# FFN1 block products, pre-added exp tiles, masks on GpSimd and wide w_in transfers in an attention + ELU-FFN kernel

## The chip, the cores and the metric

The program runs on one core of a Trainium2 chip. The metric is the device time of one execution in microseconds. A "stage" below is the time from the first FFN2 matmul of one token tile to that of the next, read from the trace.

## The reference, cut

```python
# q, k, v: 8 batches x 8 heads x 576 tokens x 64; 16 beacon keys and values in front
scores = scale * np.matmul(q, k_all.transpose(0, 1, 3, 2))      # 576 x 592
scores = np.where(causal, -1000000000.0, scores)                # beacons always visible
a = np.exp(scores - max);  a /= a.sum(-1, keepdims=True) + 1e-09
x = np.matmul(a, v_all)                                         # -> 4608 tokens x 512
h = x @ w_in                                                    # 512 x 2048    (FFN1)
g = np.where(h > 0.0, h, np.exp(np.minimum(h, 0.0)) - 1.0)      # ELU
return (g @ w_out).astype(np.float32)                           # 2048 x 512    (FFN2)
```

## The kernel before

The 4608 tokens form ten tiles: two of 256 tokens (0 and 1), then eight of 512 (2 to 9). The kernel runs every engine in a fixed order, written as a list of words. `F.b.0` means "step F on tile b, unit 0", and `z`, `b`, `c`, `d` stand for tile or batch number b-1, b, b+1, b+2. One pass through the list is a stage: FFN1 of tile b, FFN2 of tile b-1 and attention of the next batch, woven together.

FFN1 has 16 units per tile. A unit is four matmuls of 512 columns into one of two PSUM banks (tag `hps`), then exp and relu on ScalarE and one combine on VectorE, min(exp(h)-1, relu(h)), which is ELU:

```python
    def F(t, i):                                  # 16 units per 512-token tile
        h = hp[t, i] = bank("hps", name="hps") ...
        for n_ in range(512 // w):
            for cc in range(NCC):                 # 4 chunks of 128 of d_model
                nc.tensor.matmul(out=h[:, n_, :], lhsT=w_in16[:, cc, P * fc:P * (fc + 1)],
                                 rhs=xt[k][:, cc, ...], start=(cc == 0), stop=(cc == NCC - 1))
    def e(t, i):  # ScalarE:  eb = exp(h)
    def u(t, i):  # ScalarE:  rb = relu(h)
    def kk(t, i): # VectorE:  half(t, i) = min(eb - 1, rb)
```

FFN2 (step Q) already uses seven block products in place of eight (112 matmuls of 256 columns); its operand sums (Z) are on VectorE, its partial sums are copied out by step J. Softmax row sums (step L) are matmuls of the exp tiles with ones, four heads side by side, each summed over five key chunks in PSUM:

```python
    def quad(b, g, qa, qe, t, half, first):       # half is None: row sums, else value products
        for n, (j, a, e, c) in enumerate(pcs):    # key chunks
            for i in range(4):                    # four heads, 32 columns of the array each
                nc.tensor.matmul(out=t[32 * i:32 * (i + 1), ...],
                    lhsT=ones[0:kc[j], :] if half is None else v16[...],
                    rhs=ets[b, p][0:kc[j], i % 2, c:c + e - a], ...)
```

The causal masks (m) are multiplications by a triangle on VectorE. Every tile and row sum above runs in the order of the word list, one list per engine.

The softmax here doesn't subtract the row's maximum and nothing guards it: scores larger than these inputs give would overflow.

## Time and profile before

| | before |
|---|---|
| time, median (three runs; range) | 351.61 us (351.27 to 355.36) |
| first FFN2 block product (end of the start) | 105.73 us |
| stages of tiles 3, 4, 5, 6 | 35.57, 35.55, 35.55, 35.55 us |
| stages of tiles 7, 8, 9 (attention runs out) | 34.41, 26.04, 25.18 us |
| last FFN2 | 16.2 us |

The first row is the metric; the other rows are from the one profiled execution, whose span is 349.78 us, and add up to it. The prediction below shows the page lines.

### The profile page before, as it was taken

The numbers are of one execution on the slowest core, as the hardware profiler recorded it, in microseconds if no ns is written. First come the engines' busy times: TensorE is split into PE (matmuls) and PEld (weight loads), VectorE is DVE, ScalarE is ACT, GpSimd is POOL, SyncE is SP. The second block draws the span as 40 slices with busy tenths as digits, with TensorE's granted clock in tenths as the row PEclk, the third lists the DMA queues.
The fourth block names the chain that finished last, engine by engine and source line by source line (L and its number), as shares of the span: only waits on it lengthen the run. The fifth ranks groups of instructions, "written<-read, shape, count | busy, mean of one in ns | idle before, by whom it ended". The sixth has DMA issues, their size and how long they took to land.

```text
span 349.8 us, 8839 instructions
## 1 busy us (share of the span) xinstructions
PE 335.8 (96%) x3651; PEld 204.6 (59%) x3651; DVE 242.3 (69%) x514; ACT 281.2 (80%) x473; POOL 91.7 (26%) x120
## 2 busy tenths in 40 slices
PE   8887998989999999999999999999999999999995
PEld 3454655444455656656665666565665666666684
DVE  2672689689798758675867676767776767667661
ACT  1893998679868997999799979997999676777731
POOL 8877446493009107300640050000000000000000
PEclk9998999999999999999999999999999999999999
DMA  9999999999709998993799359300100010010022
GB/s 117 147 150 141 185 182 174 155 140 154 136 33 152 138 114 79 175 137 73 74 172 154 66 63 182 84 2 32 62 32 2 32 60 32 30 63 30 32 90 91
DMA packets 136232, 34.67 MB, mean 99 GB/s; under 512 B 119040, under 2 KB 135680, under 8 KB 136192
## 3 DMA queue, kind: packets, MB, share of 16 engines
q0 software_dynamic: 102080, 18.51, 67.7%
q1 hardware_dynamic: 33536, 15.47, 20.1%
q8 instruction: 28, 0.46, 0.5%
q10 hardware_dynamic: 576, 0.13, 0.2%
q14 instruction: 12, 0.10, 0.1%
HBM read 37.22 MB, written 15.34 MB: 150 GB/s over the span
## 4 chain that ended last, share of the span: by engine, by line
PE 81%; ACT 5%; DMA 4%; DVE 4%; POOL 3%; issue 1%; DVEq 0%; ACTq 0%; POOLq 0%
PE hps L432 34%; PE ops L542 28%; PE ut L322 6%; PE sc L285 6%; DMA w_in<-in_moe_w_in_dram 4%; PE lt L322 3%; PE ops L478 3%; ACT et L295 2%; ACT e L442 1%; DVE qk L259 1%; POOL kst L134 1%; POOL qst L134 1%; DVE r L464 1%; ACT r L447 1%; POOL v L147 1%
## 5 line engine op out<-in xcount | busy, mean ns | idle before, releaser
L432 PE MATMUL hps<-xT,w_in 128*128 128x512 f16 (+1 forms) x640 | 148.9, 359 | 3.9 <-DMA w_in<-in_moe_w_in_dram 2.5
L457 DVE SCALAR_TENSOR_TENSOR gt<-e,r 128x512 f16<-128x512 f32 x133 | 92.0, 692 | 59.2 <-ACT r L447 54.3
L442 ACT ACTIVATE e<-hps 128x512 f32<-128x512 f32 x144 | 89.3, 621 | 33.7 <-PE hps L432 32.6
L295 ACT ACTIVATE et<-sc 128x832 f16<-128x832 f32 x128 | 106.0, 897 | 2.7 <-PE sc L285 2.6
L542 PEld LDWEIGHTS <-gt 128*128 128x128 f16 x768 | 75.1, 98 | 29.0 <-issue 0.3
L447 ACT ACTIVATE r<-hps 128x512 f16<-128x512 f32 x133 | 82.8, 624 | 5.0 <-PE hps L432 2.5
L432 PEld LDWEIGHTS <-w_in 128*128 128x128 f16 x640 | 56.5, 98 | 50.0 <-issue 7.4
L542 PE MATMUL ops<-wt,gt 128*128 128x256 f16 x384 | 52.5, 273 | 0.0
L542 PE MATMUL ops<-w_out,gt 128*128 128x256 f16 x384 | 51.4, 273 | 0.0
L311 DVE TENSOR_TENSOR et<-et,triu 128x256 f16<-128x256 f16 (+2 forms) x164 | 41.8, 357 | 13.2 <-ACT et L295 11.0
L147 POOL DMA_DIRECT2D v<-in_v_dram x40 | 35.5, 977 | 5.7 <-DMA w_out<-in_moe_w_out_dram 1.7
L499 DVE TENSOR_TENSOR gt<-gt 128x1024 f16<-128x1024 f16 x48 | 32.5, 683 | 0.0
L322 PE MATMUL ut<-et,v 128*32 128x464 f16 (+4 forms) x672 | 23.6, 283 | 1.0 <-DVE qk L263 1.0
L396 DVE TENSOR_TENSOR xT<-ut,rl 128x448 f16<-128x448 f32 (+7 forms) x56 | 22.3, 452 | 2.8 <-ACT rl L364 2.3
L322 PEld LDWEIGHTS <-v 128*32 128x32 f16 (+1 forms) x800 | 17.4, 98 | 11.5 <-issue 4.8
L285 PE MATMUL sc<-qkd 64*128 64x208 bf16 (+5 forms) x320 | 21.5, 252 | 0.0
L142 POOL DMA_DIRECT2D v<-in_beacon_v_dram x8 | 4.3, 536 | 60.1 <-PE ut L322 57.2
L551 ACT COPY sm<-ops 128x512 f32<-128x512 f32 x24 | 16.0, 667 | 5.0 <-PE ops L542 5.0
L558 DVE TENSOR_TENSOR osb<-ops,sm 128x512 f32<-128x512 f32 x24 | 16.4, 683 | 4.3 <-issue 3.7
L285 PE MATMUL sc<-qk 64*128 64x208 bf16 (+10 forms) x208 | 15.4, 246 | 2.8 <-ACT et L295 2.5
L542 PE MATMUL ops<-w_out,s 128*128 128x256 f16 x128 | 17.6, 273 | 0.0
L285 PEld LDWEIGHTS <-qkd 64*128 64x128 bf16 x320 | 11.3, 94 | 10.4 <-issue 8.2
(59 smaller groups left out, 257.3 us busy)
## 6 DMA issues: line engine op xcount, KB each, us to landing
out_dram<-osb SPq DMA_DIRECT2D x36, 256.0 KB, 2.3
v<-in_v_dram POOLq DMA_DIRECT2D x24, 128.0 KB, 6.9
scr<-in_k_dram POOLq DMA_DIRECT2D x5, 576.0 KB, 17.1
scr<-in_q_dram POOLq DMA_DIRECT2D x5, 576.0 KB, 10.3
w_in<-in_moe_w_in_dram POOLq DMA_DIRECT2D x16, 128.0 KB, 6.8
w_out<-in_moe_w_out_dram POOLq DMA_DIRECT2D x4, 512.0 KB, 9.9
v<-in_v_dram POOLq DMA_DIRECT2D x8, 112.0 KB, 5.7
v<-in_v_dram POOLq DMA_DIRECT2D x8, 80.0 KB, 7.0
```

Of the source, the lines that this page charges most:

```text
L147: nc.gpsimd.dma_start(out=vt[b][r0:r0 + n, j, :, :], in_=v[b, :, ilo[j]:ilo[j] + n, :].rearrange("h s d -> s h d"),)
L285: nc.tensor.matmul(out=s[:, h, a - c0:e - c0], lhsT=t[D * h:D * (h + 1), 1, P * j:P * (j + 1)], rhs=t[D * h:D * (h + 1), 0, NB + qa + a - ...
L295: nc.scalar.activation(out=ets[b, p][:, :, GW * g:GW * (g + 1)], in_=sc[b, p, g][:, :, 0:GW], func=AFT.Exp, bias=0.0, scale=SCALE)
L311: nc.vector.tensor_tensor(out=o, in0=o, in1=triu[0:kc[j], :, t0:t0 + e - a], op=ALU.mult)
L322: nc.tensor.matmul(out=t[32 * i:32 * (i + 1), a - qa:e - qa], lhsT=ones[0:kc[j], :] if half is None else v16[0:kc[j], j, h, 32 * half:32 * ...
L396: nc.vector.tensor_tensor(out=x_tile(k)[:, cc, tok - TT * k:to - TT * k], in0=u[:, o:o + to - tok], in1=r[:, o:o + to - tok], op=ALU.mult)
L432: nc.tensor.matmul(out=h[:, n_, :], lhsT=w_in16[:, cc, P * fc:P * (fc + 1)], rhs=xt[k][:, cc, a - TT * k:e - TT * k], start=(cc == 0), sto ...
L442: nc.scalar.activation(out=eb[t, i], in_=flat(hp[t, i]), func=AFT.Exp, bias=0.0, scale=1.0)
L447: nc.scalar.activation(out=rb[t, i], in_=flat(hp[t, i]), func=AFT.Relu, bias=0.0, scale=1.0)
L457: nc.vector.scalar_tensor_tensor(out=half(t, i), in0=eb[t, i], scalar=1.0, in1=rb[t, i], op0=ALU.subtract, op1=ALU.min)
L499: nc.vector.tensor_tensor(out=o_, in0=a_, in1=b_, op=op_)
L542: nc.tensor.matmul(out=xy[t, n_][:, qd, :], lhsT=lw[:, P * qd:P * (qd + 1)], rhs=wt_[:, c, :], start=(first and qd == 0 and c == 0), stop= ...
```

## The change

Intent: take work off TensorE, which sets the end, and put it on engines with room.

- In tiles 4 to 9, three groups of four of the 16 FFN1 units become seven block products each: 28 matmuls of 256 columns in place of 16 of 512. The products accumulate in two PSUM banks; partial sums are copied out and added (K), so h appears in SBUF or in PSUM, and ELU is formed as max(h, min(exp(h), 1) - 1), with the clamp on GpSimd (U).
- Exp tiles are added over key chunks 1 to 4 (D) so that a row-sum group needs 8 matmuls, not 24.
- Some masks (m with `.p`), operand sums and chunk adds go to GpSimd.
- w_in arrives in 16 transfers, each 1024 columns wide (before, 512); the start is reordered, and q and k are staged in fixed buffers.

```diff
-        f_ = slice(512 * c, 512 * (c + 1))
+        f_ = slice(DF // 2 * c, DF // 2 * (c + 1))
         for g in range(2):
-            for t in range(2):
-                nc.gpsimd.dma_start(out=w_in16[:, 2 * g + t, f_], in_=wi_v[:, :, g, t, f_])
+            for i in range(4):
+                nc.gpsimd.dma_start(
+                    out=w_in16[32 * i:32 * (i + 1), 2 * g:2 * g + 2, f_], in_=wi_v[i, :, g, :, f_])
 ... [masks]
+                nc.gpsimd.affine_select(
+                    out=o, in_=o, compare_op=ALU.is_ge, fill=0.0, base=t0,
+                    pattern=[[0, 2], [1, e - a]], channel_multiplier=-1)
 ... [D_: chunk adds]
+        (nc.vector if eng == "v" else nc.gpsimd).tensor_tensor(
+            out=o, in0=t[0:rows, :, a:e] if n == 0 else o, in1=t[0:rows, :, col:col + e - a], op=ALU.add)
 ... [row sums of batches from BD on]
+                    nc.tensor.matmul(
+                        out=t[32 * i:32 * (i + 1), a:e], lhsT=ones,
+                        rhs=(presum if a else ets)[k][:, i % 2, a:e],
+                        start=True, stop=True, skip_group_check=True)
 ... [seven products, partial sums, exp, clamp, maximum]
+    ring = {"hs": [0, fr[0:2]], "sm": [0, fr[2:4]]}
+    def P_(t, g, ph):           # 4 matmuls of 256 columns
+    def K_(t, g, ph, eng="s"):
+        if ph in (0, 2, 3):
+            (nc.scalar.copy if eng == "s" else nc.vector.tensor_copy)(out=fm[t, g, ph], in_=src)
+        else:
+            nc.vector.tensor_tensor(out=hb[t, g, ph], in0=src, in1=fm[...], op=ALU.add)
+    def E_(t, g, ph):           # ScalarE exp of hb (ph 6: of PSUM)
+    def U_(t, g, ph):
+        if ph == 6:
+            nc.scalar.activation(out=r_, in_=hsrc(t, g, ph), func=AFT.Relu, bias=0.0, scale=1.0)
+        else:
+            nc.gpsimd.tensor_scalar(
+                out=r_, in0=eb[t, g, ph], scalar1=1.0, scalar2=1.0, op0=ALU.min, op1=ALU.subtract)
+    def V_(t, g, ph):           # VectorE: max(hb, clamp); ph 6: the old combine
 ... [new word lists: the start; BODY3 (tile 3, makes the weight sums H); BODY (4 to 7); TAIL (8, 9)]
```

## The prediction

> **What bounds the kernel now.** I read the page's busy shares and slices first, then the chain of waits that ended last, then the stages by window, then the timeline of one stage, then GpSimd's and VectorE's timelines side by side.
>
> ```profile
> PE 335.8 (96%) x3651; PEld 204.6 (59%) x3651; DVE 242.3 (69%) x514; ACT 281.2 (80%) x473; POOL 91.7 (26%) x120
> PE   8887998989999999999999999999999999999995
> PE 81%; ACT 5%; DMA 4%; DVE 4%; POOL 3%; issue 1%; DVEq 0%; ACTq 0%; POOLq 0%
> L432 PE MATMUL hps<-xT,w_in 128*128 128x512 f16 (+1 forms) x640 | 148.9, 359 | 3.9 <-DMA w_in<-in_moe_w_in_dram 2.5
> ```
>
> TensorE is busy for 96%, carries 81% of the chain, and what idle it has lies in the first third. So two regions have to be treated apart: a start with holes and a steady part without. The windows (columns: window; length, PE, weight loads, DVE, ACT, POOL busy; clock; DMA share; GB/s) say the same:
>
> ```profile
> 20.00:30.00 10.00, 6.47 (x139) 4.12 (x139) 6.21 (x14) 6.75 (x12) 7.01 (x11) 0.99 1.35 142
> 178.00:213.00 35.00, 35.00 (x383) 21.38 (x378) 24.82 (x55) 32.36 (x56) 5.88 (x11) 1.00 1.14 115
> 284.50:317.00 32.50, 32.50 (x222) 21.47 (x221) 22.10 (x35) 24.05 (x46) 0.00 (x0) 1.00 0.10 34
> ```
>
> From about 106 us on, the program repeats one stage per 512-token tile: FFN1 of tile b, FFN2 of tile b-1 and attention of the next batch; the last two FFN1 tiles have no attention. The chain gives the period and the cost of each piece (start, length):
>
> ```profile
> 182.17 0.82 PE lt L322 x24
> ...
> 204.51 0.97 PE hps L432 x4
> 206.25 0.86 PE hps L432 x4
> ...
> 217.72 0.82 PE lt L322 x24
> ...
> 332.99 13.01 PE ops L542 x119
> ```
>
> The row sums of the same group come 217.72 - 182.17 = 35.55 us apart, all of it TensorE work. A 512-column matmul costs 0.86/4 = 0.216 us, a 256-column one 13.01/119 = 0.109 us, and one group's row sums (24 matmuls, four column groups side by side, 1664 columns) 0.82 us.
>
> ScalarE and VectorE are pipelined, so their cost is the distance of starts, not the length shown:
>
> ```profile
> 249.27 0.69 DVE L457 SCALAR_TENSOR_TENSOR gt<-e,r 128x512 f16<-128x512 f32 x1 [0.34 <-ACT r L447]
> 249.88 0.69 DVE L499 TENSOR_TENSOR gt<-gt 128x1024 f16<-128x1024 f16 x1
> 250.49 0.66 DVE L311 TENSOR_TENSOR et<-et,triu 128x224 f16<-128x224 f16 x2
> 251.19 0.62 ACT L447 ACTIVATE r<-hps 128x512 f16<-128x512 f32 x1
> 251.67 1.65 ACT L295 ACTIVATE et<-sc 128x832 f16<-128x832 f32 x2
> 253.16 0.65 ACT L442 ACTIVATE e<-hps 128x512 f32<-128x512 f32 x1
> ```
>
> VectorE: 0.61 us for 512 fp32 elements or for 1024 fp16 ones. ScalarE: 0.48 us for 512 elements, (253.16 - 251.67)/2 = 0.745 us for a softmax exp of 832. Three masks of 256 fp16 elements ran in 0.63 us, some 0.2 us each.
>
> **What the Trainium skill says.** (1) "TensorE: Matmul & The Clock Gate", Back-to-back issue gap: N/2.4 + 2.5 ns; that is 0.216 and 0.109 us, and the trace agrees to the nanosecond. So halving a matmul costs only some 2.5 ns, and fewer streamed columns are time won. (2) "VectorE: DVE Perf Modes", the perf-mode tier table: tensor_tensor runs at two elements per cycle in 16 bits and one in fp32; the 0.61 us for both sizes agree. (3) "SBUF — State Buffer", Who interferes with whom: a VectorE instruction with two SBUF inputs and a GpSimd instruction that reads SBUF exclude each other for the whole instruction. The trace shows it once, plainly:
>
> ```profile
> 77.76 3.66 POOL L585 COPY qkd<-bkT 128x32 bf16<-128x32 bf16 x1
> 79.74 0.68 DVE L499 TENSOR_TENSOR wt<-w_out 128x1024 f16<-128x1024 f16 x1
> 80.34 0.43 DVE L311 TENSOR_TENSOR et<-et,triu 128x256 f16<-128x256 f16 x2
> 80.70 0.68 DVE L499 TENSOR_TENSOR wt<-w_out,wt 128x1024 f16<-128x1024 f16 x1
> 81.30 0.68 DVE L485 COPY osb<-ops 128x512 f32<-128x512 f32 x1
> ```
>
> A 32-element copy that needs 0.21 us elsewhere took 3.66 us, and ended at 81.42, as soon as VectorE went to an instruction that reads PSUM alone. (4) "GPSIMD Engine Reference", Elementwise: 4497 ns for a two-input fp32 add of 2048, so 2.2 ns per element. No two-input operation runs on GpSimd in the kernel before.
>
> **The change, part by part.**
>
> Block products (tiles 4 to 9, three groups of four of the 16 FFN1 units). Each group: 16 matmuls of 512 columns become 28 of 256. Per tile 48 x 0.216 = 10.37 us become 84 x 0.109 = 9.2 us, so 1.2 us less; six tiles 7.0 us. All of it lies on the engine that sets the end. The price is on the others. Per group there were 4 exp, 4 relu (ScalarE) and 4 combines (VectorE). Now there are 3 ScalarE copies of partial sums, 4 exp and 1 relu (again 8 operations); on VectorE 3 adds from PSUM and 4 combines; and 3 clamps on GpSimd.
>
> Row sums. With chunks 1 to 4 added ahead, one group streams 112 + 464 = 576 columns and not 1664: 0.82 x 576/1664 = 0.28 us, so 0.54 us less, twice per batch, for batches 3 to 7: 5.4 us. The adds are 16 fp16 instructions per batch on VectorE or GpSimd.
>
> Sum on TensorE: 7.0 + 5.4 = 12.4 us: 2.25 us in each of the stages of tiles 4 to 7 (35.55 to 33.3), 1.1 in that of tile 3, 1.2 in each of the last two FFN1 tiles.
>
> Do the others keep up with 33.3 us? Counted from the built program's order, per stage of tiles 4 to 7:
> - ScalarE: 12 exp, 3 relu, 8 copies, 8 exp and relu of the plain quarter, 3 output copies = 34 x 0.48 = 16.3; 16 softmax exps x 0.745 = 11.9; 4 normalisers at about 0.55 = 2.2. Sum 30.4 us (before 31.4).
> - VectorE: 37 operations at about 0.6 (16 combines, 10 partial sums, 7 FFN2 operand sums, 4 outputs) = 22.2; 8 masks x 0.2 = 1.6; 9 chunk adds 3.3; 4 x differences 1.3; scaling 2.8. Sum 31.2 us (before about 23).
> - GpSimd, estimates: 9 clamps at about 0.63 (its two select instructions took 0.29 us for 128 and 0.40 us for 256 elements, extrapolated), 12 selects x 0.4 = 4.8, 7 chunk adds 7.5 and one operand sum 2.3 at the skill's 2.2 ns, copies 0.5: about 21 us that read SBUF; with some 8 us of DMA issue about 29 us.
>
> None exceeds 33.3 alone, but all stand at 87 to 94%, in strict order, with only two PSUM banks for a group and a ring of two for the partial sums. Each product must wait until the partial sum two products back has been copied out. I allow 1 us lost per stage of tiles 4 to 7, 4 us in all. In the stage of tile 3 VectorE has 24 weight sums (0.2 each), 16 chunk adds and 20 masks beside its old work: about 35 us, so its 1.1 us is lost too.
>
> The start. TensorE's work there hardly changes. Before, it is held from 27 to 31 us for w_in, which comes in column quarters; now half of all columns come in eight wide transfers, behind more of q and k, and scores of batch 1 lie before the first FFN1. The holes for w_in are about 5 us; I take 3 us as won, plus or minus 4.
>
> Result: 351.6 - 12.4 + 1.1 + 4 - 3 = 341.3; I say 341.
>
> **Rivals.** First, the shared port becomes the bound. Per stage VectorE has about 20 us of two-SBUF-input work (combines, operand sums, masks, chunk adds) and GpSimd about 21 us of reads. If they exclude each other wholly, that is 41 us against 33.3, partly hidden only under VectorE's 11 us from PSUM. Each of four stages would grow by 3 to 5 us over 35.55, and the time would be 355 to 370. For it: the 3.66 us copy. Against: the clamp's and selects' lengths are extrapolated, reads may be over before an instruction ends, the order puts GpSimd's work beside PSUM adds, and VectorE waiting for a clamp leaves the port free. Second, the copy-out of partial sums becomes TensorE's wait: the stages stay near 35.5, and only the start and the last tiles show a gain, 345 to 350. For it: a product of four matmuls takes 0.44 us, its copy about 0.67 us plus queueing. Against: FFN2 products and scores stand between the products. Third, all engines follow, and the start closes its holes: 333 to 337.
>
> **Range and chances.** The main path gives 336 to 345 and is the likeliest; the second rival lies within 2% and the first above it. With 344.6 as the limit for a gain of 2%: faster 0.66, within 2% 0.19, slower 0.15. Range 332 to 357.
>
> **What would show it.** Right: stages of tiles 4 to 7 some 34 us long with TensorE over 95% busy; row-sum groups of about 0.28 us; 84 products per stage at 0.109 us. The first rival: GpSimd's clamps and adds far longer than 0.6 to 2 us, VectorE's combines waiting for a clamp, TensorE idle for VectorE. The second: TensorE idle in front of products, released by ScalarE's or VectorE's copy-out. The start is right if FFN2's first block product comes at about 103 us, not 106, and no matmul waits for w_in. I would be wrong above all if GpSimd's share in a stage nears 100%.

## More of the kernel before

One more row of the windows, the whole stage of tile 5, is the yardstick for everything that follows (columns: window in us; length; busy us and instructions of PE, weight loads, VectorE, ScalarE, GpSimd; granted clock; DMA share; GB/s):

```profile
176.85:212.40 35.55, 35.55 (x385) 21.64 (x384) 25.21 (x56) 32.91 (x57) 7.03 (x11) 1.00 1.14 114
```

TensorE is busy for the whole stage, ScalarE for 93%, VectorE for 71%; GpSimd hardly works.

## The result, and the profile after

| | before | after |
|---|---|---|
| time, median of four runs each on the same chip | 351.44 us (351.2 to 355.36) | 428.36 us (427.39 to 429.62) |
| span of the profiled execution | 349.78 | 427.92 |
| first FFN2 block product | 105.73 | 101.13 |
| stages of tiles 3, 4, 5, 6 | 35.57, 35.55, 35.55, 35.55 | 38.10, 53.10, 53.11, 52.25 |
| stages of tiles 7, 8, 9 | 34.41, 26.04, 25.18 | 45.79, 37.95, 30.34 |

The changed kernel is correct and much slower: ratio 1.217, 95% interval 1.209 to 1.225. A ratio here is the mean time of one kernel's fast runs over that of the other's of the same rounds, so it is not quite the ratio of the medians that are quoted.

The 78.1 us between the two profiled spans divide as: start -4.6, stage of tile 3 +2.5, stages of tiles 4 to 7 +63.2, last two tiles +17.1 (differences of the rows above). So the start did what it should, and each stage with block products lost 5 to 18 us. One wait of the start before, in which matmuls wait for w_in (us in total, times, longest), is gone after:

```profile
PE hps L432 <- DMA w_in<-in_moe_w_in_dram: 2.5, 2, 1.3
```

The page after (busy shares; the chain of waits by engine; the largest GpSimd group, with busy us, mean ns of one and the idle time before it):

```profile
PE 351.5 (82%) x3700; PEld 230.2 (54%) x3700; DVE 351.8 (82%) x630; ACT 278.9 (65%) x455; POOL 275.0 (64%) x258
...
POOL 34%; PE 25%; DVE 19%; ACT 12%; issue 8%; DMA 1%; DVEq 0%; ACTq 0%; POOLq 0%
L681 POOL TENSOR_SCALAR r<-e 128x512 f16<-128x512 f32 x54 | 108.8, 2032 | 68.6 <-ACT e L672 67.1
```

TensorE fell from 96% busy to 82% and from 81% of the chain to 25%; GpSimd, 26% busy before, now leads the chain with 34%. Its clamps alone are 54 instructions of 2.03 us mean; GpSimd spent another 67.1 us waiting for their input. An engine that is waiting and leading the chain at once is part of a loop, not simply overloaded. By stage (tile 3, tile 5, tile 9; same columns as above):

```profile
101.13:139.23 38.10, 34.98 (x354) 21.22 (x352) 34.63 (x88) 33.93 (x57) 19.72 (x18) 1.00 1.02 95
...
192.33:245.44 53.11, 39.89 (x389) 26.52 (x388) 46.27 (x69) 33.62 (x55) 45.35 (x43) 0.89 0.77 79
...
381.43:411.76 30.33, 25.25 (x206) 19.91 (x204) 25.39 (x38) 17.85 (x32) 19.93 (x10) 1.00 0.11 36
```

In the middle row VectorE is busy 46.3 us and GpSimd 45.4, where I had counted 31 and 29. TensorE's 39.9 us are not more work, since it streams fewer columns than in the old stage; the granted clock was 0.89 here, and 1.00 in the stages of tiles 3 and 9. What lowered it, and what share it has in the loss, was not tested. The waits (waited for; us in total, times, longest) name the loop:

```profile
POOL r L681 <- ACT e L672: 67.1, 20, 9.7
...
DVE gt L694 <- POOL r L681: 20.5, 30, 1.8
PE hps L650 <- DVE kst L663: 17.6, 10, 5.3
PE hps L650 <- DVE qst L663: 17.3, 9, 5.3
```

A product (L650) waits up to 5.3 us for VectorE's addition of a partial sum (L663), the exp (L672) waits for that sum, the clamp (L681) for the exp, VectorE's maximum (L694) for the clamp; and VectorE, in strict order, reaches the next partial sum only after that maximum. A piece of the chain of waits in tile 5's stage shows it (start, length, what):

```profile
225.79 0.54 ACT e L672
...
232.14 1.89 POOL r L681
234.03 1.68 POOL et L322 x3
...
235.90 1.94 POOL r L681
...
237.87 1.94 DVE gt L694
```

The last line is a maximum that takes 0.68 us where GpSimd is idle. The timeline beside it shows why (start, length, engine, line, operation):

```profile
220.87 2.63 DVE L351 TENSOR_TENSOR qk<-et 128x928 f16<-128x928 f16 x1 [0.58 <-POOL et L322]
221.07 1.93 POOL L351 TENSOR_TENSOR qk<-et 128x928 f16<-128x928 f16 x1
...
237.80 2.83 POOL L351 TENSOR_TENSOR qk<-qk,et 128x672 f16<-128x672 f16 x2
237.87 1.94 DVE L694 TENSOR_TENSOR gt<-qst,r 128x512 f16<-128x512 f32 x1 [0.25 <-POOL r L681]
```

A chunk add of 0.63 us (the median of this form) became 2.63 us on VectorE beside a GpSimd add: the exclusion on the shared port that the prediction quoted from the Trainium skill, "SBUF — State Buffer", Who interferes with whom. The trace agrees here. (In the lines that the prediction shows, only GpSimd's copy waited; VectorE's instructions kept their lengths.)

So there are three suspects: the clamp's own length, the port, and a dependence loop with engines too full to run ahead. They have to be told apart by experiments.

### The profile page after: what moved, and what is told of

Read it like the earlier page. It is cut to its first block, busy times and chain, and to the rows that moved or that the text cites. A ratio compares the mean times of both kernels' runs of the same rounds, so it can differ in the third digit from the quotient of the medians.

```text
span 427.9 us, 9235 instructions
## 1 busy us (share of the span) xinstructions
PE 351.5 (82%) x3700; PEld 230.2 (54%) x3700; DVE 351.8 (82%) x630; ACT 278.9 (65%) x455; POOL 275.0 (64%) x258
## 4 chain that ended last, share of the span: by engine, by line
POOL 34%; PE 25%; DVE 19%; ACT 12%; issue 8%; DMA 1%; DVEq 0%; ACTq 0%; POOLq 0%
POOL r L681 19%; PE hps L468 7%; ACT et L303 6%; PE ops L578 5%; POOL et L322 5%; DVE gt L493 4%; POOL qk L351 3%; POOL gt L535 3%; PE hps L650 3%; PE ops L514 3%; DVE gt L694 3%; PE sc L293 2%; DVE gt L535 2%; POOL scr L710 2%; ACT e L672 2%
## 5 line engine op out<-in xcount | busy, mean ns | idle before, releaser
L681 POOL TENSOR_SCALAR r<-e 128x512 f16<-128x512 f32 x54 | 108.8, 2032 | 68.6 <-ACT e L672 67.1
L468 PE MATMUL hps<-xT,w_in 128*128 128x512 f16 (+1 forms) x352 | 72.9, 346 | 9.3 <-DVE kst L663 3.5
L660 ACT COPY kst<-hps 128x512 f32<-128x512 f32 x46 | 26.9, 589 | 40.7 <-PE hps L650 40.3
L468 PEld LDWEIGHTS <-w_in 128*128 128x128 f16 x352 | 32.4, 99 | 37.2 <-issue 14.6
L483 ACT ACTIVATE r<-hps 128x512 f16<-128x512 f32 x56 | 33.7, 610 | 27.8 <-PE hps L468 19.9
L478 ACT ACTIVATE e<-hps 128x512 f32<-128x512 f32 x72 | 43.7, 610 | 3.2 <-PE hps L468 1.6
L493 DVE SCALAR_TENSOR_TENSOR gt<-e,r 128x512 f16<-128x512 f32 x56 | 42.6, 779 | 1.8 <-ACT r L483 1.4
L650 PEld LDWEIGHTS <-w_in 128*128 128x128 f16 x288 | 27.9, 105 | 26.2 <-issue 13.4
L320 DVE TENSOR_TENSOR et<-et,triu 128x256 f16<-128x256 f16 (+3 forms) x119 | 34.5, 323 | 5.3 <-ACT et L303 4.1
L694 DVE TENSOR_TENSOR gt<-qst,r 128x512 f16<-128x512 f32 x27 | 28.0, 1036 | 12.2 <-POOL r L681 12.1
L694 DVE TENSOR_TENSOR gt<-kst,r 128x512 f16<-128x512 f32 x27 | 29.8, 1105 | 8.5 <-POOL r L681 8.4
L650 PE MATMUL hps<-xT,w_in 128*128 128x256 f16 x144 | 24.7, 310 | 9.4 <-DVE kst L663 4.7
L650 PE MATMUL hps<-qst,lo 128*128 128x256 f16 x72 | 12.0, 294 | 21.3 <-DVE kst L663 11.1
L672 ACT ACTIVATE e<-kst 128x512 f32<-128x512 f32 x27 | 17.1, 634 | 16.6 <-DVE kst L663 16.5
L322 POOL TENSOR_SCALAR_AFFINE_SELECT et<-et 128x256 f16<-128x256 f16 (+2 forms) x45 | 27.2, 624 | 0.0
L650 PE MATMUL hps<-qst,w_in 128*128 128x256 f16 x144 | 23.7, 291 | 4.2 <-DVE qst L663 2.3
```

Of the source, the lines that this page charges most:

```text
L320: nc.vector.tensor_tensor(out=o, in0=o, in1=triu[0:kc[j], :, t0:t0 + e - a], op=ALU.mult)
L322: nc.gpsimd.affine_select(out=o, in_=o, compare_op=ALU.is_ge, fill=0.0, base=t0, pattern=[[0, 2], [1, e - a]], channel_multiplier=-1)
L478: nc.scalar.activation(out=eb[t, i], in_=flat(hp[t, i]), func=AFT.Exp, bias=0.0, scale=1.0)
L493: nc.vector.scalar_tensor_tensor(out=half(t, i), in0=eb[t, i], scalar=1.0, in1=rb[t, i], op0=ALU.subtract, op1=ALU.min)
L650: nc.tensor.matmul(out=hx[t, g, n_][:, c, :], lhsT=lw, rhs=rh, start=(first and c == 0 and k_ == 0), stop=(k_ == 1), skip_group_check=True)
L681: nc.gpsimd.tensor_scalar(out=r_, in0=eb[t, g, ph], scalar1=1.0, scalar2=1.0, op0=ALU.min, op1=ALU.subtract)
```

## The experiments

Besides the changed kernel seventeen ran. The times of sixteen and of after, medians of two to six fast runs, each beside the kernel before on the same chip:

| kernel | median us | before | ratio (95% interval) | stage of tile 5, us | result |
|---|---|---|---|---|---|
| after | 428.36 | 351.44 | 1.217 (1.209 to 1.225) | 53.11 | correct |
| clamp_one | 411.83 | 352.63 | 1.168 (1.158 to 1.178) | 50.79 | correct |
| clamp_vector | 406.34 | 351.06 | 1.156 (1.150 to 1.163) | 50.06 | correct |
| rest_vector | 398.27 | 351.06 | 1.133 (1.120 to 1.146) | 44.53 | correct |
| no_gpsimd | 388.50 | 352.63 | 1.102 (1.095 to 1.110) | 44.47 | correct |
| selects_only | 381.96 | 352.63 | 1.084 (1.078 to 1.091) | 43.60 | correct |
| clamp_scalar | 378.21 | 351.06 | 1.076 (1.069 to 1.083) | 41.67 | correct |
| products_only | 375.28 | 352.44 | 1.065 (1.062 to 1.067) | 40.61 | correct |
| no_clamp | 368.55 | 352.45 | 1.045 (1.038 to 1.051) | 39.19 | wrong |
| presum_late | 352.98 | 352.44 | 1.001 (0.995 to 1.006) | 37.20 | correct |
| plain_presum | 352.08 | 352.63 | 0.998 (0.992 to 1.004) | 36.87 | correct |
| no_clamp_products | 349.11 | 352.45 | 0.989 (0.979 to 1.000) | 35.34 | wrong |
| ring_four | 348.30 | 352.45 | 0.987 (0.981 to 0.994) | 35.35 | wrong |
| copy_early | 347.75 | 352.14 | 0.989 (0.983 to 0.996) | 35.48 | wrong |
| narrow_w | 346.71 | 352.44 | 0.984 (0.982 to 0.985) | 35.55 | correct |
| start_only | 344.75 | 352.44 | 0.979 (0.974 to 0.984) | 35.55 | correct |
| sums_short | 341.81 | 352.45 | 0.969 (0.963 to 0.974) | 35.03 | wrong |

The seventeenth, alone, is the kernel before with a measurement behind its last product; its single time (407.63 us, state unknown) means nothing.

### First call: what a clamp costs, and clamp against port

**alone.** GpSimd instructions of the change by themselves, then beside VectorE.

```diff
+    for _ in range(4):  gp.tensor_scalar(out=so[:, 0:512], in0=f_, scalar1=1.0, scalar2=1.0, op0=min, op1=subtract)
+    ...                 # the same from fp16; copies; selects; adds of 928; clamps again
+    for _ in range(16): nc.vector.tensor_tensor(out=y[0], in0=y[1], in1=y[2], op=ALU.add)   # beside 4 clamps
+    for _ in range(16): nc.vector.tensor_copy(out=y[0][:, 0:512], in_=pz)                   # beside 6 clamps
```

> The kernel before with a bench behind its last product: clamps (min, then subtract) of 512 fp32 elements, of 512 fp16 elements, plain copies, selects of 256 and chunk adds of 928 on GpSimd with VectorE idle; then clamps beside VectorE adds with two SBUF inputs, then beside VectorE copies from PSUM. Theory A (the clamp itself is long): 1.9 us alone, and about the same beside PSUM copies. Theory B (the shared port makes it long): about 0.6 us alone and beside PSUM copies, 2 us or more only beside two-input adds. The output stays right; the whole is longer than 351 us by the bench, some 60 to 90 us.

GpSimd's and VectorE's timelines (start, length of the whole row, count at the end):

```profile
358.32 2.64 POOL L676 CAST s<-bk 128x512 f16<-128x512 f32 x4
...
362.73 5.35 POOL L681 TENSOR_TENSOR s<-s 128x928 f16<-128x928 f16 x3
368.17 7.92 POOL L683 TENSOR_SCALAR s<-bk 128x512 f16<-128x512 f32 x4
376.05 9.31 POOL L689 TENSOR_SCALAR s<-bk 128x512 f16<-128x512 f32 x4
377.24 12.45 DVE L687 TENSOR_TENSOR w_in<-w_in 128x1024 f16<-128x1024 f16 x16
```

A clamp alone takes 1.92 us, from fp32 or fp16 alike (four start to finish in 7.92 us); a copy of the same 512 elements 0.61 us; a select of 256 elements 0.41; an add of 928 fp16 elements 1.73, so 1.87 ns per element. My 0.63 us for the clamp was right for a copy and three times too small for a min followed by a subtraction. The add was sized well: the 2.2 ns per element that I took from the Trainium skill was on the safe side.

The last two rows correct the picture of the port. By their single records, three of the clamps beside VectorE's two-input adds took 2.38 us, and during each of these two adds ran in their usual 0.69 us and one in 0.98. That is a mild mutual cost in this bench, not exclusion for the length of a clamp. Beside VectorE copies from PSUM neither side lost anything (six clamps in 12.01 us, sixteen copies at 0.69). So the exclusive hold is seen for GpSimd's two-input adds, and not for its clamps. It can be worse inside the kernel: in after, at 202.02 us, a mask on VectorE (224 elements, two SBUF inputs) took 1.22 us beside a clamp, where the shortest of its kind takes 0.26.

**clamp_scalar.** Clamps become relu on ScalarE, the combine is the old one; GpSimd keeps adds, masks and sums.

```diff
-        if ph == 6:
+        if True:                                   # relu on ScalarE, for every product
             nc.scalar.activation(out=r_, in_=hsrc(t, g, ph), func=AFT.Relu, bias=0.0, scale=1.0)
```

> The changed kernel with all 54 clamps as relu on ScalarE, as the seventh product already has it; selects and chunk adds stay on GpSimd. Theory A (clamp length in the chain add, exp, clamp, max): 355 to 370 us, stages of tiles 4 to 6 at 36 to 40 us instead of 53. Theory B (port exclusion through selects, adds and sums): still above 395, stages above 45. Theory C (TensorE waits for copy-outs of partial sums through two PSUM banks, whatever engine clamps): above 410.

Measured: 378.21 us, 50 us less than after, between the ranges of A and B. No other single move of work in this call gave as much (22 and 30 us below), so the clamp on GpSimd is the largest single cause, but not the only one.

**clamp_vector.** The same clamp instruction on VectorE.

```diff
-            nc.gpsimd.tensor_scalar(
+            nc.vector.tensor_scalar(
                 out=r_, in0=eb[t, g, ph], scalar1=1.0, scalar2=1.0, op0=ALU.min, op1=ALU.subtract)
```

> The same with the clamps on VectorE: 9 more operations of 0.4 us a stage there. Theory A: 360 to 375 us. Theory B: above 395, because VectorE's clamp too needs the shared port. Theory C: above 410.

Measured: 406.34 us, only 22 us less, in the range of theory B. On VectorE a clamp takes 0.42 us in the median, yet the stages of tiles 4 and 5 stay at 50 us: VectorE is then held in its order by waits for exps (19.6 us in all, 21 times), and by GpSimd: VectorE instructions beside its adds are stretched, and one clamp took 4.33 us (192.18 to 196.51) while GpSimd was issuing DMA transfers. So B has a part in this one, and A alone does not explain it. A short clamp does not suffice where the engine that gets it is in the same loop.

**rest_vector.** The clamps stay on GpSimd; its masks, chunk adds and operand sums go to VectorE, so hardly any two-input work is left there.

```diff
+            args = ["v" if a == "p" else a for a in args]
             t = b + "zbcd".index(n_) - 1 if n_ in "zbcd" else n_
```

> The changed kernel with every select, chunk add and operand sum of the repeated stages back on VectorE; only the clamps stay on GpSimd. Theory A: 405 to 425 us, because the clamp chain stays, and the tail stages (38 and 30 us) do not move. Theory B: 360 to 385 us, because GpSimd then reads for 17 us a stage only and VectorE is seldom shut out. Theory C: as now, 428.

(The x differences of three words keep their default, GpSimd.) Measured: 398.27 us, 30 us less; stages of tiles 4 to 6 at 44.5 to 45.5. This lies between the ranges of A and B. So taking GpSimd's other work away gains about 8 us a stage, through the port and through GpSimd's queue. The two cuts (50 and 30 us) do not add up: together they give 40 (next).

The traces show how much the port does to VectorE directly. For each VectorE instruction of tile 5's stage, take its length less the shortest of the same line and shape in that trace, and add these up: 13.1 us in after, of which 7.3 on instructions that ran mostly beside GpSimd's two-input adds, 3.4 beside clamps and 2.1 beside selects. The sum is 2.6 us in rest_vector, 0.6 in no_gpsimd and 0.5 in the kernel before. With adds and selects on GpSimd but no clamps there it is 3.8 (clamp_scalar) and 6.3 (no_clamp, below). How much of the 13.1 us reaches the end of the stage was not tested.

### Second call: what else is in the stage

**no_gpsimd.** The edits of clamp_scalar and rest_vector together.

> Clamps on ScalarE and all selects, chunk adds and operand sums of the repeated stages on VectorE: GpSimd is left with DMA issue, small copies and the four x differences of the stage of tile 3. If clamp length and port exclusion are additive causes, VectorE's own sum decides, 31.2 + 5.6 = 37 us a stage: stages 37 to 39 us, total 358 to 366. If the copy-outs of partial sums (theory C) hold TensorE even so, the stages stay at 41 to 42 us as in the run with the clamps on ScalarE, and the total stays above 373.

Measured: 388.5 us, 10 us more than clamp_scalar; the sum of VectorE's work (358 to 366 us) did not decide. The window of tile 5's stage:

```profile
183.29:227.76 44.47, 37.76 (x390) 25.42 (x388) 38.62 (x89) 37.59 (x65) 9.87 (x12) 0.94 1.00 95
```

GpSimd does nothing of the change any more, and no engine is full: the largest is VectorE, 38.6 of 44.5 us. What is left is waiting of each for the others in fixed order.

**selects_only.** As no_gpsimd, but the masks stay on GpSimd (`if f in "DZX"` ahead of the replacement).

> As no_gpsimd, but the 12 selects of a stage stay on GpSimd (0.41 us each when alone). If long two-input adds hold the port and short selects hardly do, this is a little better than no_gpsimd, 354 to 362, since VectorE is spared 2.4 us a stage. If every GpSimd read shuts VectorE out, or the selects wait in strict order behind DMA issue, it is worse, 365 to 375.

Measured: 381.96 us. Neither range was met, but masks on GpSimd are a gain: 6.5 us less than on VectorE.

**clamp_one.** The clamp with one operation, min; the subtraction goes into VectorE's maximum.

```diff
-                out=r_, in0=eb[t, g, ph], scalar1=1.0, scalar2=1.0, op0=ALU.min, op1=ALU.subtract)
+                out=r_, in0=eb[t, g, ph], scalar1=1.0, scalar2=None, op0=ALU.min)
...
+            eng.scalar_tensor_tensor(out=o_, in0=v_(rb[t, g, ph]), scalar=1.0, in1=v_(hb[t, g, ph]), op0=ALU.subtract, op1=ALU.max)
```

> The changed kernel with GpSimd's clamp cut to one operation (min with 1); the subtraction goes into VectorE's combine, which stays one instruction. The plain copy took 0.61 us alone and the two-operation clamp 1.92. If the second operation makes the clamp slow, it takes 0.6 to 1.1 us and the time falls to 385 to 400; if the element type or any scalar operation does, it stays near 1.9 us and 425.

Measured: 411.83 us, between the two forecasts. One operation takes at least 1.48 us and 1.70 in the median, so the second operation is not what makes it long. The time follows the clamp's length: some 0.22 us less on each of 54 clamps (12 us by count) took away 16.5 us.

**plain_presum.** No block products; the old order with the new start, the pre-added exp tiles (all adds on VectorE) and short row sums.

```diff
-    BODY3 / BODY / TAIL
+    BODY = old order, D.b.n after the masks of each chunk, L.b.0 after F.b.3, L.b.1 after F.b.10
```

> The new start and the row sums over added chunks, but no block products and no GpSimd selects: FFN1 in plain 512-column matmuls in the old order, chunk adds on VectorE. TensorE saves 1.1 us a stage in five stages and starts the first stage some 5 us earlier: 340 to 343 us, faster than both kernels. If the chunk adds come late and TensorE waits for them, about 346; if VectorE's 5.5 us more a stage bind, 350 or more.

Measured: 352.08 us; stages 36.87, so 1.3 us longer than the old 35.55 although TensorE streams less. Against sums_short below, which has the same short row sums and no adds, a stage is 1.84 us longer, and 1.40 of that lie at the row sums: TensorE waits for VectorE's chunk adds (0.92 us idle at one place).

### Third call: each part by itself

**start_only.** The new start with the old steady part: no products, no chunk adds, old row sums, old masks.

```diff
-        if half is None and b >= BD:
+        if half is None and b >= NT:               # old row sums
...
+            if f == "D":
+                continue
```

> The changed kernel's start (order, wide w_in transfers, q and k staging) in front of the old stages: plain FFN1, row sums over all chunks, masks on VectorE, no chunk adds, no block products of FFN1. The first FFN2 block product comes at 98 to 101 us instead of 105.7, the stages stay at 35.55: 343 to 347 us. If the old stages do not take up the gain, because the start only moves work behind that point, 350 to 352.

Measured: 344.75 us over six runs (343.47 to 347.14), against 352.44: ratio 0.979 (0.974 to 0.984). The stages are the old ones to 0.02 us; that of tile 5:

```profile
170.29:205.84 35.55, 35.55 (x386) 21.62 (x385) 25.23 (x56) 32.91 (x57) 9.89 (x12) 1.00 1.38 115
```

This is the part of the change that pays, and this correct kernel is faster than both kernels; whether by over 2% the interval leaves open.

**narrow_w.** start_only with w_in in narrow transfers of 512 columns, in the new place.

```diff
-            for i in range(4):
-                nc.gpsimd.dma_start(out=w_in16[32 * i:32 * (i + 1), 2 * g:2 * g + 2, f_], in_=wi_v[i, :, g, :, f_])
+            for t in range(2):
+                for o_ in (0, 512):                # f5: the 512 columns from o_ on
+                    nc.gpsimd.dma_start(out=w_in16[:, 2 * g + t, f5], in_=wi_v[:, :, g, t, f5])
```

> start_only with w_in in the old shape, 128 rows by 512 columns in each of 16 transfers, in the same two bursts. If the wide shape is what shortens the start, 2 us or more are lost again; if the order of the steps does it, within 1 us of start_only.

Measured: 346.71 us. Matmuls (1.5 us in all) and weight loads (2.2 us) wait for w_in in this one and not in start_only, but 2 us lie inside the scatter: the first FFN2 product of kernels with the same start (but for the chunk adds of one batch, which some leave out) falls anywhere between 97.5 and 103.3 us. Most of the gain is there with narrow transfers too; what the width adds stays open.

**products_only.** Block products with clamps on ScalarE, no chunk adds, old row sums, nothing of the change on GpSimd.

> Block products with the clamps on ScalarE, without chunk adds and with all masks and operand sums on VectorE. By the sums VectorE then has 31 us and ScalarE 34.7 us a stage, TensorE 34.4. If the sum on the fullest engine decides, stages of 35.5 to 37.5 us and 350 to 358 in all; if the waits from product to copy-out to product decide, whatever the loads, 40 us a stage or more and above 370.

Measured: 375.28 us, tile 5's stage 40.61. A window of one stage's length, from within tile 4's stage into tile 5's (both take 40.61 us):

```profile
175.00:215.60 40.60, 36.14 (x428) 25.15 (x431) 31.84 (x70) 36.52 (x65) 10.18 (x12) 1.00 1.00 100
```

With ELU in its old form the products give ScalarE eight operations more than before (65 and 57 in the windows): 36.5 us of work, more than the whole old stage. That alone rules this form out.

**presum_late.** plain_presum with the row sums placed later, so that the adds have longer.

> plain_presum with the second group's row sums moved back by one FFN1 unit and the first group's adds moved ahead of the combine, so that TensorE does not wait for chunk adds (1.25 us and 0.47 us a stage in that run). If those waits were all, stages of 35 us, 340 to 344 us. If the waits only move, no better than start_only.

Measured: 352.98 us, stages 37.2. The waits only change place (PE's timeline, two rows of one stage):

```profile
182.12 0.37 PE L365 MATMUL lt<-qk,ones 128*32 128x464 f16 x2 [0.61 <-DVE qk L351]
...
200.34 0.35 PE L293 MATMUL sc<-qst 64*128 64x160 bf16 x4 [1.24 <-DVE xT L432]
```

### Fourth call: are the gains there if their price is waived?

These kernels compute a wrong result. They show what TensorE would gain if the others cost nothing.

**no_clamp.** The clamps of after are dropped: the maximum takes the exp itself. GpSimd keeps masks, adds and sums.

```diff
-        r_ = rb[t, g, ph] = melt.tile([P, 512], FP16, tag="r", name="r")
+        if ph != 6:
+            rb[t, g, ph] = eb[t, g, ph]
+            return
```

> The changed kernel with the 54 clamps left out and VectorE's max taking exp itself (wrong result on purpose): GpSimd keeps selects, chunk adds and operand sums. The clamp's whole cost shows. If the port exclusion by the others is small, it comes near 350 to 360 (stages of 35 to 38 us); with the exclusion real it stays at 365 to 380, like the run with the clamps on ScalarE (378).

Measured: 368.55 us; stages 41.6, 39.2 and 40.2. Without the clamps 60 of the 77 us are gone. The 4 to 6 us per stage that remain over 35.5 belong to the rest: the chunk adds, masks and sums on VectorE and GpSimd.

**no_clamp_products.** no_clamp, with the rest moved to VectorE, no chunk adds and the old row sums: block products alone, without clamps.

> products_only with the clamps left out (wrong result on purpose): ScalarE falls from 34.7 to 30.4 us a stage, VectorE stays at 31, GpSimd does nothing. If ScalarE's strict order and load made the 40.6 us stages, they fall to 35 to 37 and the whole to 350 to 358. If the hand-over product, copy-out, product through two PSUM banks makes them, they stay above 39 and the whole above 366.

Measured: 349.11 us; tile 5's stage 35.34, as long as before but for 0.2 us. It is the old length at last, but the 1.2 us that the products should save is not there. The PE timeline shows both halves of the answer:

```profile
211.11 0.60 PE L650 MATMUL hps<-qst,lo 128*128 128x256 f16 x4
...
212.10 0.61 PE L650 MATMUL hps<-qst,w_in 128*128 128x256 f16 x4
213.17 0.60 PE L650 MATMUL hps<-xT,hi 128*128 128x256 f16 x4 [0.46 <-DVE kst L660]
213.61 0.93 PE L578 MATMUL ops<-w_out,gt 128*128 128x256 f16 x7
```

From 213.17 to 213.61 four matmuls take 0.44 us, 0.110 each: the product itself is as short as predicted. But from 212.10 to 213.17 it is 1.07 us, 0.63 more than four matmuls need: the product waits until VectorE (L660) has copied out the partial sum two products back, once per stage. So the wait is 0.63 of the 1.0 us that is missing. Counted by starts, row sums and value products take another 0.2 us, as the two no longer stand side by side in the order (4.85 us a stage, 4.65 before), and TensorE leaves its full array form for a smaller one twelve times a stage, not eleven, which is 0.1 us more.

**ring_four.** no_clamp_products with four buffers for partial sums, not two.

```diff
-    ring = {"hs": [0, fr[0:2]], "sm": [0, fr[2:4]]}
+    ring = {"hs": [0, fr[0:2] + more], "sm": [0, fr[2:4]]}     # more: two unused buffers
```

> no_clamp_products with four buffers instead of two for the partial sums that exp and max read (wrong result on purpose, too). If the ring of two is what makes TensorE wait, 1 us or more a stage is won; if the PSUM banks or the order are, nothing (within 1 us in all).

Measured: 348.3 us, stages 35.35, the same wait. The ring of two is not the limit.

**sums_short.** start_only with short row sums that read one exp tile, no adds at all.

```diff
-                        rhs=(presum if a else ets)[k][:, i % 2, a:e],
+                        rhs=ets[k][:, i % 2, a:e],
```

> start_only with the short row sums (576 columns a group) but no chunk adds, so the sums leave chunks out (wrong result on purpose): what TensorE gains if the adds cost nothing. By my prediction 2 x 0.54 us a stage, stages of 34.5 us and some 339.5 in all; if eight small matmuls with their changes of weights take near 0.5 us and not 0.28, half of that.

Measured: 341.81 us; stages 35.03, 0.52 us less than start_only's, where I had predicted 1.08. By the starts in the trace, row-sum and value matmuls together take 3.69 us in a stage, and 4.65 in start_only: 0.96 is saved, near the prediction. But each stage now has a wait that was not there:

```profile
192.22 0.53 PE L293 MATMUL sc<-qst 64*128 64x416 bf16 x6 [0.37 <-DVE xT L432]
```

TensorE reaches the scores earlier and waits for VectorE's scaling. Nearly half of the saving is given back there: these scores start 0.43 us late.

### Fifth call: is that one wait the order's fault?

**copy_early.** no_clamp_products with the copy that is waited for moved ahead of a mask and an operand sum in VectorE's order.

```diff
-    ... P.b.0.3 m.b.1.1 lt.c.0 U.b.0.1 ... P.b.0.4 x.b.2.2 Z.z.1.1 K.b.0.3.v K.b.0.4 ...
+    ... P.b.0.3 K.b.0.3.v m.b.1.1 lt.c.0 U.b.0.1 ... P.b.0.4 x.b.2.2 Z.z.1.1 K.b.0.4 ...
```

> no_clamp_products (no clamp, nothing of the change on GpSimd, old row sums; wrong on purpose) with one VectorE copy of a partial sum (third product of the first group) moved ahead of a mask and an FFN2 operand sum in VectorE's order. In that kernel a product waits once per stage, 0.63 us beyond the usual distance, for this copy. If the seven-product scheme's gain on TensorE is real and only this place in the order ate it, the stages of tiles 4 to 6 fall from 35.34 to about 34.7 us and no product waits for the copy. If TensorE's time per product is itself longer than counted, or the wait only moves to the next product, they stay at 35.2 to 35.4.

Measured: 347.75 us, stages 35.48, not 34.7. The wait for the copy is gone; in its place a later product starts 0.49 us late, in wait for VectorE's next partial sum (L663 in the waits), and the one after it 0.27 us late. The wait moved, as the second of my two readings had it. A single edit of the order does not free it. Whether a full new search of the order would, stays open.

## Why the prediction was wrong, point by point

**What bounds the kernel before** was read correctly: 35.55 us stages of pure TensorE work.

**The start** was right in direction and rather low in size: I took 3 us as won, plus or minus 4, and the first FFN2 product at about 103 us. It came at 101.1 us, and start_only, which has nothing else of the change, gained 7.7 us by its medians and 6.6 by its profiled span. No matmul waits for w_in any more, as predicted; but narrow_w, where some still do, has most of the gain too, so the reason is shown only in part.

**TensorE's own terms** were nearly right: 0.109 us per matmul inside a product (0.110 measured) and, for the row sums, 1.08 us a stage (0.96 measured). (The section of the Trainium skill that the formula came from calls it the gap of an isolated matmul and gives shorter ones for a stream at 512 columns; here it held in the stream, at 0.216 us.) What failed is the assumption that TensorE's saving is the stage's saving. In no_clamp_products it was 0.2 us and not 1.2, in sums_short 0.5 and not 1.1, because TensorE then waited for VectorE (0.63 us and 0.43 us); 0.3 us of the first loss are changes of order and array form that were not counted.

**The step that failed first** is "9 clamps at about 0.63 (its two select instructions took 0.29 us for 128 and 0.40 us for 256 elements, extrapolated)". The clamp takes 1.92 us by itself. Nine are 17.3 us per stage and not 5.7, which takes GpSimd's count from about 29 to about 41 us, over the 33.3 us target. I carried the length of one kind of instruction over to another; the trace of before held no GpSimd tensor_scalar to check it on. That the clamps are the main cause is shown: without them 60 of the 77 us go (no_clamp), moved to ScalarE 50 (clamp_scalar), though moved to VectorE only 22 (clamp_vector). GpSimd was busy for 45.4 of 53.1 us (85%), so not near the 100% that I had named as the sign: the clamp hurt more by its length in the chain than by filling the engine.

**The second step that failed** is "None exceeds 33.3 alone, [...] I allow 1 us lost per stage of tiles 4 to 7". Tile 5's stage lost 17.6 us over the old length. The sum of busy times did not bound this chain through four engines: product, partial sum on VectorE, exp on ScalarE, clamp on GpSimd, maximum on VectorE, with each engine in a fixed order. Even in no_gpsimd, with no engine above 38.6 us of work, the stage took 44.5. And ScalarE, had it taken the clamps, would have been over the limit by itself (36.5 us in products_only).

**The stage of tile 3** I put at no gain and no loss. It took 2.5 us more; 1.2 of them are there without chunk adds (36.78 us in no_clamp_products), the rest come with the adds.

**The rivals.** The first, the shared port, was named with the right signs, GpSimd's instructions "far longer than 0.6 to 2 us" and TensorE idle for VectorE, but sized at 3 to 5 us per stage. The port is real: a chunk add of 0.63 us took 2.63, and VectorE's instructions were stretched by 13.1 us in tile 5's stage. Moving GpSimd's two-input work away gave 30 us (rest_vector), which includes the shorter queue on GpSimd. But the rival put the clamps' reads into the port as much as the adds', and those cost less: 0.29 us a clamp in alone, 3.4 of the 13.1 us in the stage. The second rival, the copy-out of partial sums as TensorE's wait, with stages near 35.5, is in the main what no_clamp_products shows; it was hidden behind the larger loss.

**The chances.** Both estimates that carried the 0.66 for a gain (the clamp's length and the 1 us allowance) had no measurement behind them, and no case that I weighed had the first one off by a factor of three.

## What to carry to other kernels

Before work moves to an engine, measure the exact instruction there, with its operations and types; here a different instruction of that engine was no substitute, and the chain that passed through the slow one repeated its length at each turn. A saving on the busiest engine counted here only as far as the next engine could run ahead of it: waive the price once, on purpose, as in no_clamp_products and sums_short, to see what the best case is worth before building it. Take a many-part change apart early; here the one part that paid was the reordered start.

## What the Trainium skill lacked or had wrong

- "GPSIMD Engine Reference", Engine selection, says that GpSimd is about two times slower for two-input operations and "1-input is roughly line-rate". For a plain copy of 512 elements that may pass (0.61 us), but a one-input clamp with two operations took 1.92 us (3.75 ns per element) and with one operation 1.48 to 1.70, where VectorE took 0.42 for the two-operation form. The page has no figure for tensor_scalar.
- The same page, Elementwise: 4497 ns for a two-input fp32 add of 2048 elements, by my estimate 2.2 ns per element. No fp16 figure is given; 928 fp16 elements took 1.73 us here, 1.87 ns per element.
- "SBUF — State Buffer", Who interferes with whom: the pair is held "for the whole instruction". That agrees with GpSimd's two-input adds (a VectorE add of 0.63 us became 2.63) and not with its clamps: while a clamp lasted 2.38 us, two of three VectorE adds kept their 0.69 us and one took 0.98. Inside the kernel it was once more than that: a VectorE mask of 0.26 us took 1.22 beside a clamp.
- "TensorEngine Tiling (Array Packing)", Key Properties, says that a change of tiling mode drains TensorE, without a figure. Here a 256-column full-array matmul followed by a score, row-sum or value matmul took 0.202 to 0.205 us to the next start, and 0.109 where none followed: some 0.095 us for a switch, eleven times in a stage before. The way back cost about the same: 0.202 us from a 256-column score matmul to the next FFN1 matmul.
